# Three tiles for normed tokens and attention output, one gathered V unit, and crossings that wait in TensorE's own stream

## The chip, the cores and the metric

One NeuronCore of a Trainium2 chip runs the whole kernel. Times are device microseconds of that core. TensorE (PE) multiplies, VectorE (DVE), ScalarE (ACT) and GpSimd (POOL) work on elements, SyncE (SP) and ACT issue DMA transfers. Each engine runs its own instruction stream in order, and the streams meet at semaphores: an instruction waits until counters that other engines raise have reached a value. "PEld" in the profile is TensorE's loading of the stationary operand, "PEq", "POOLq" and so on are the sequencers that read the streams.

## The reference, cut to what matters

```python
def A(x, wqkv, wo):                       # B, S, D = 1, 2048, 448; H, Dh = 16, 28
    q, k, v = split(x @ wqkv)             # [B, H, S, Dh] each
    idx = pos[:, None] - 2 * arange(8)    # each position sees itself and 7 earlier ones, 2 apart
    logits = where(idx >= 0, einsum('bhsd,bhswd->bhsw', q, k[idx]) * Dh ** -0.5, -1e9)
    return einsum('bhsw,bhswd->bhsd', softmax(logits), v[idx]).merge_heads() @ wo

def B(x, w1, w2):                         # 448 -> 1792 -> 448
    return silu(x @ w1) @ w2

sa, ca, ga, sb, cb, gb = split(silu(c) @ w_mod, 6)
x = x + ga * A(layernorm(x) * (1 + ca) + sa)
x = x + gb * B(layernorm(x) * (1 + cb) + sb)
```

All inputs are bf16. A position only sees positions of its own parity, so the tokens are handled as two sequences of 1024 (`NP`), one for each parity, side by side.

## The kernel before

**Layout.** Activations stand transposed in SBUF: features on the partitions, positions along the free axis. The 448 features take four blocks of 128 rows (`KT`), and a parity is an index of its own. One tile, `ho` (L176), holds two things: the normed tokens `hT` in its columns 512 to 1535, and the attention output `oT` in its columns 0 to 1023. They overlap on purpose: output position 512 lies where token 0 was, once the tokens of the first half are no longer read.

**Tokens.** Chunks of 256 positions per parity are normed (`Pair`), transposed by a DMA into `hT` and scaled and shifted there (`h_later`; the `mod` operations at L236 and L238).

**Products.** A contraction over 448 is made of 64-row pieces. `pair` (L418) makes each product in two groups. The straight group (`.S`) runs two halves of TensorE's rows at once, 8 products for an output of two banks; the crossing group (`.C`), 6 products, adds the other half's pieces into the same two banks with the halves exchanged. A crossing may only start when its straight group's last product is through. `signal` (L215) sees to that: an empty instruction on GpSimd waits for that product, and the crossing's first weight load and its second product wait for GpSimd. Between a straight group and its crossing the order puts a group of another pair.

`project(k)` makes Q and K of chunk k (L483: `qk{k}{g}`, g = 0 to 3). `project_v(u)` makes V for unit u (L500: `v{u}`), 64 keys of each of two blocks, two parities: stationary operands of 64x64.

**Attention.** A unit u is two blocks of 57 queries with 64 keys each (starts in `Q0` and `K0`); there are nine. Logits (`lg{u}`, L538), exponentials on ACT (`ex{u}0`, `ex{u}1`, L545), mask on DVE (`mk{u}`, L596), product with V (`av{u}`, L612), reciprocal and normalization on DVE (`rc{u}`, `on{u}`, L619 and L624), a transposing DMA from `o` into `op` (`otr{u}`, L627), and `align` (`al{u}`, L633, L636 and L637), which copies `op` to its 114 columns of `oT`. Align of a unit that reaches past position 512 must wait until the projections have read the tokens there: the list `late` (L647).

**Output projection and FFN.** `out_proj(m)` (`wo{m}`, L663) multiplies 128 positions of `oT` by `wo`, which DVE scales by the gate ga once that is computed (L342, L345, L793); wo needs the aligns that cover its columns. Then come the second norm and the FFN (L692, L697, L717), in four chunks, and the stores.

**Order.** Every piece of work is an operation of a `Plan` with its dependencies. A table of numbers, `ORDER`, fixes the order by hand: a number is the operation's place in the list of creation, the letter its engine (p TensorE, a ACT, v DVE, g GpSimd, s SP). The framework derives semaphore waits from which instructions write and read which tile.

Of the kernel before, what the change touches and what calls it, by code (L numbers as in the profile page):

```python
# [15 lines left out]
D = 448  # L16
# [4 lines left out]
KT = 4  # L21
# [12 lines left out]
WARM, JUNK = 6, 22  # L34
HOW1 = "bbbbbbbb"
# [4 lines left out]
2a 25a 58a 59p 60a 0s 30g 33g 68v 69v 1s 26g 70g 74v 75v 76g 71v 4s 35p 54p 72a 6a 73a 39p 51s 37p 44p 42p 50p 40s 41s 9s 52s 53s 43s 3s 117v 116v  # L40
118g 77v 78a 8a 79a 110v 111v 62p 80p 83p 63v 81v 29g 84v 85v 82a 10a 5s 55s 102p 7s 119g 11a 120a 121a 47s 45s 123s 56s 112g 28g 113g 27g 64v 114v
103g 106p 115v 122s 107g 61v 67v 65v 104p 108p 49s 12s 14s 66a 98p 174v 173v 105a 109a 94p 99g 95g 175g 48s 100p 176v 167v 168v 169g 36s 46s 57s 38s
216v 170v 96p 97a 90p 91g 86p 87g 101a 15s 13s 124a 171v 127v 92p 125v 126v 88p 93v 177v 172v 178v 215v 132p 34g 133g 128p 89a 129g 31g 255p 256a 257a
130p 134p 135a 140p 131v 136p 264p 258v 137g 141g 32g 265a 16a 266a 142p 138p 210v 209v 211g 139a 143v 148p 149g 259p 150p 144p 179s 17s 180s 184a
267v 268p 260v 261v 262s 18s 145g 212g 181a 151a 269v 183v 182v 146p 156p 152p 147a 217g 157v 270v 218v 153v 219v 220v 185p 213a 214a 186g 278p 279a
280a 189p 190g 158v 281v 187p 191p 201p 188a 202g 271s 292p 192a 272v 159v 293a 203p 282p 222s 294a 221s 283v 284v 21a 193p 194g 285s 197p 195p 223v
225v 263a 204a 198g 226v 224v 199p 273p 235p 200v 274g 236g 295v 196a 306p 307a 308a 275p 276v 277v 286a 237p 238v 205p 206g 348g 349a 20s 296p 207p
287p 288g 231p 289p 232g 233p 350a 351g 297v 309v 298v 208a 299s 290v 291v 310p 243p 352g 244g 355v 247p 248g 19s 234a 356a 357a 358g 359g 245p 249p
246a 227p 311v 353v 354v 312v 320p 228g 250a 229p 300v 321a 322a 301p 239p 360v 361v 230a 302g 303p 362s 323v 305v 313s 304v 442v 251p 324p 314a 252g
253p 363s 22s 240g 23a 254a 241p 242a 325v 326v 367v 315p 154p 316g 444a 155a 334p 335a 336a 366v 364v 365v 317p 319v 392p 393g 318v 337v 384p 388p  # L50
394p 443a 338p 161v 339v 395a 385g 386p 445g 389g 390p 387a 368p 380p 327s 328v 340v 449v 381g 24s 166v 160v 163v 369g 372p 450a 451a 370p 373g 374p
382p 391a 371a 341s 329p 452g 330g 375a 383a 162v 164v 165v 376p 331p 377g 446g 378p 332v 333v 447v 405p 342a 379a 343p 344g 453g 454v 455v 414p 345p
347v 346v 406p 407p 415a 416a 417v 448v 428p 429a 430a 431v 457s 396p 397p 398p 418p 432p 515g 508g 408g 509a 516a 399g 400p 401p 402p 517a 510a 419v
433v 420v 456s 518g 519v 520v 458a 409p 511g 434v 461v 459v 512v 460v 513a 521a 514a 410p 411p 421s 474p 466p 467g 475g 422a 403v 412v 470p 471g 476p
435s 468p 477a 469a 472p 473a 462p 423p 424g 478p 479g 522s 523s 527a 463g 425p 436v 427v 426v 574v 526v 480p 481a 437p 464p 482p 438g 486p 439p 487g
465a 525a 524a 483g 484p 441v 440v 581v 485a 583a 544p 488p 545g 546p 489a 490p 532p 491p 499p 500p 492p 533g 534p 576a 575a 582a 584g 585g 586v 547a
587a 548p 549g 577g 535a 501p 528p 502g 493g 529g 578v 550p 551a 579v 580v 588s 589s 592v 404s 494p 495p 496p 552p 530p 531a 497v 503p 504p 536p 505p
622v 593a 590a 537g 538p 540p 591a 553g 506v 541g 554p 542p 539a 555a 594p 598p 595g 596p 599g 543a 597a 600p 601a 602p 565p 603g 566p 567p 604p 605a
498s 556p 568g 610p 569p 570p 614p 611g 571p 615g 572v 557p 616p 617a 612p 606p 618p 558p 607g 507s 613a 559g 619g 608p 609a 560p 620p 623p 625p 626p
621a 627p 561p 562p 563v 564s 624v 413s 573s 628g 629p 630p 631p 634p 635p 636p 637p 638p 632v 639v 640s 641v 642s 633s 643v 644a  # L60
# [81 lines left out]
def layer(ctx, tc, io, safe):  # L142
# [33 lines left out]
    ho = ct([128, 2, KT, NP + 512], "ho")  # L176
    hT = ho[:, :, :, 512:512 + NP]
    oT = ho[:, :, :, 0:NP]
# [7 lines left out]
    vb = [ct([128, 2, H, 32], f"v{i}") for i in range(NV)]  # L186
    pb = [ct([128, H * 2 * QB], f"p{i}") for i in range(NPB)]
# [7 lines left out]
    scr = ct([128, D], "scr")  # L195
# [19 lines left out]
    def signal(name, first, ends):  # L215

        def f(o):
            ends["sig"] = G.nop()
            after(ends["sig"], ends["last"])
        return P.op(name, "g", "signal", f, [first])  # L220

    P = Plan()
    for r, n in (("ps", 4 if ORDER and not safe else 3), ("v", NV), ("p", NPB), ("xn", NX), ("ob", NO), ("op", NST), ("out", 3)):
        P.resource(r, n)
# [126 lines left out]
    class Pair:  # L351

        def __init__(self, name, m, src, how, after=()):
# [12 lines left out]
            def total(o, t):  # L366
                S.activation(out=scr[:], in_=x_all[:, us[t], :], func=ACTF.Identity, accum_out=sums[:, us[t]:us[t] + 1])
# [4 lines left out]
            def square(o, t):  # L372
                S.activation(out=scr[:], in_=x_all[:, us[t], :], func=ACTF.Square, bias=mv[:, t, 0:1], accum_out=mv[:, t, 1:2])  # L373
# [44 lines left out]
    def pair(name, kind, mma, mmb, deps, evacs, mode="P", take=()):  # L418
# [3 lines left out]
        def run(o, way):  # L422
            t = ps[first["slot"]["ps"][0]]
            ks = STEPS[way]
            for n, (ka, kb) in enumerate(ks):
                stop = way == 1 and n == len(ks) - 1
                for j in ((0, 1) if way == 0 else (1, 0)):
                    hf = j if way == 0 else 1 - j
                    i = (mma, mmb)[j](t, half(hf), kb if hf else ka, way == 0 and n == 0, stop)
                    if way == 1 and n == 0 and j == 1:  # L430
                        after(i[0], ends["sig"])
            if way == 0:
                ends["last"] = i[-1]
        first = P.op(f"{name}.S", "p", kind + "S", lambda o: run(o, 0), deps, take=("ps",) + take, group=(mode, name, 0))
        sig = signal(f"{name}.g", first, ends)
        second = P.op(f"{name}.C", "p", kind + "C", lambda o: run(o, 1), [first, sig], group=(mode, name, 1))
# [10 lines left out]
    def h_first(i, nrm):  # L447
# [10 lines left out]
        def mod(o, a):  # L458
            for k in (2 * a, 2 * a + 1):
                affine(o, hT[:, :, k, 128 * i:128 * i + 128], views[a][:, k % 2], modc[:, 1, k:k + 1], modc[:, 0, k:k + 1])  # L460
# [6 lines left out]
    def h_later(k, nrm):  # L467
        trs = [nrm[i].transpose(hT[:, :, :, 256 * k + 128 * i:256 * k + 128 * i + 128].rearrange("p t k s -> p (t k) s"), ()) for i in range(2)]
        out_ = []
        for kt in range(KT):  # L470
            v = hT[:, :, kt, CP * k:CP * k + CP]
# [3 lines left out]
    def project(k):  # L475
# [3 lines left out]
        for g in range(4):  # L479
            def mm(j, g=g):  # L480
                def f(t, rows, kt, start, stop):
                    w = wp[rows, kt, H * j + 4 * g:H * j + 4 * g + 4, :].rearrange("p h d -> p (h d)")
                    return [matmul(t[:, j, :], lhsT=w, rhs=hT[rows, :, kt, s0:s0 + CP], start=start, stop=stop)]  # L483
# [10 lines left out]
    def project_v(u):  # L494

        def mm(j):
            k0 = K0[2 * u + j]

            def f(t, rows, kt, start, stop):
                return [matmul(t[half(par), j, 0:D], lhsT=hT[rows, par, kt, k0:k0 + KB], rhs=wv[rows, kt, :], start=start, stop=stop) for par in range(2)]  # L500
# [5 lines left out]
        deps = []  # L506
        for m in range(K0[2 * u] // 128, (K0[2 * u + 1] + KB - 1) // 128 + 1):
# [394 lines left out]
```

## Time and profile before

| what | us |
|---|---|
| median of 3 runs | 175.22 |
| lowest and highest | 174.96, 177.31 |
| the profiled execution | 176.32 |
| its span, first to last instruction | 174.6 |
| TensorE busy in it | 158.5 |
| mean granted TensorE clock in it | 0.967 of full |

The profile's times are those of the one profiled execution. A row of a timeline gives start, duration, engine, source line, operation, what it writes and reads, count, and in brackets the idle time before it and what ended that. A row of the waits reads "engine, output and line, what it waited for: total us, times, longest". Products overlap in TensorE, so that a product's own duration is longer than the distance to the next.

### The profile page before, as it was taken

How to read it: one execution, taken by the hardware profiler on the slowest of the kernel's cores; microseconds unless marked ns; L12 is line 12 of the kernel's file. 1: busy time of each engine (PE TensorE's matmuls, PEld its weight loads, DVE VectorE, ACT ScalarE, POOL GpSimd, SP SyncE). 2: the span in 40 equal slices, each digit the busy share in tenths (PEclk: the TensorE clock that was granted, in tenths of full speed). 3: DMA queues.
4: the chain of work that ended last, by engine and by line, in shares of the span. 5: the costliest groups of instructions: out<-in, count | busy, mean ns of one | idle time of the engine just before them, and what ended most of it. 6: DMA issues, size and time to landing. Idle time of an engine off the chain costs nothing. (4 is left out here: it accounts for less than half of the span.)

```text
span 174.6 us, 6087 instructions
## 1 busy us (share of the span) xinstructions
PE 158.5 (91%) x2684; PEld 81.8 (47%) x2684; DVE 84.2 (48%) x188; ACT 102.4 (59%) x136; POOL 24.2 (14%) x66
## 2 busy tenths in 40 slices
PE   3669999999668998999999999999999999999950
PEld 1264454655334454554456544445444444445540
DVE  3589688985573737669265950330144000202220
ACT  3348587979463587798888588786426730440000
POOL 7450432310000220030112400002200000000000
PEclk9956999999996999999999999999999999999998
DMA  4979899587930395973022462000151100000402
GB/s 139 345 252 238 169 361 130 161 109 163 168 100 4 58 193 112 307 224 60 4 63 61 59 137 54 4 0 0 29 147 53 56 0 0 4 0 0 163 31 86
DMA packets 33453, 18.51 MB, mean 106 GB/s; under 512 B 25102, under 2 KB 33422, under 8 KB 33422
## 3 DMA queue, kind: packets, MB, share of 16 engines
q1 hardware_dynamic: 30208, 14.46, 36.4%
q10 hardware_dynamic: 3214, 3.61, 6.9%
q8 instruction: 22, 0.36, 0.9%
q14 instruction: 9, 0.07, 0.2%
HBM read 10.21 MB, written 1.84 MB: 69 GB/s over the span
## 5 line engine op out<-in xcount | busy, mean ns | idle before, releaser
L697 ACT ACTIVATE both<-ps 128x1024 bf16<-128x1024 f32 x28 | 27.8, 1021 | 24.5 <-PE ps L692 24.5
L717 PE MATMUL ps<-w,both 64*128 64x448 bf16 x392 | 39.9, 349 | 0.0
L483 PE MATMUL ps<-ho,wp 64*128 64x512 bf16 x224 | 26.8, 377 | 3.4 <-ACT ho L633 3.4
L692 PEld LDWEIGHTS <-w 64*128 64x128 bf16 x392 | 19.0, 94 | 21.9
L717 PEld LDWEIGHTS <-both 64*128 64x128 bf16 x392 | 18.8, 94 | 18.2
L692 PE MATMUL ps<-wqk,w 64*128 64x512 bf16 x196 | 23.3, 376 | 0.0
L692 PE MATMUL ps<-h,w 64*128 64x512 bf16 x196 | 23.1, 376 | 0.0
L545 ACT ACTIVATE p<-ps 128x912 bf16<-128x912 f32 x18 | 15.8, 928 | 5.9 <-PE ps L538 4.4
L483 PEld LDWEIGHTS <-wp 64*128 64x128 bf16 x224 | 10.5, 94 | 16.0 <-issue 5.1
L500 PE MATMUL ps<-wv,ho 64*64 64x448 bf16 x252 | 17.1, 407 | 0.0
L671 DVE SCALAR_TENSOR_TENSOR x_all<-ps,x_all 128x448 bf16<-128x448 f32 x16 | 9.4, 623 | 15.8 <-PE ps L663 15.8
L663 PE MATMUL ps<-wo,ho 64*128 64x448 bf16 x112 | 13.3, 350 | 0.5 <-DVE ho L633 0.5
L487 ACT CAST qk<-ps 128x1024 bf16<-128x1024 f32 x11 | 11.0, 1019 | 4.4 <-PE ps L483 4.4
L395 ACT ACTIVATE xn<-x_all,nm,rs 128x512 bf16<-128x512 bf16 x12 | 9.1, 806 | 7.3 <-DVE nm L383 6.8
L373 ACT ACTIVATE scr<-x_all,mv 128x448 bf16<-128x448 bf16 x16 | 10.7, 668 | 3.3 <-POOL mv L370 3.0
L397 DVE TENSOR_SCALAR xn<-x_all,mv,rs 128x512 bf16<-128x512 bf16 x20 | 7.3, 403 | 9.9 <-POOL rs L377 9.9
L377 POOL TENSOR_TENSOR rs<-rs,negh 128x2 f32<-128x2 f32 x16 | 11.8, 735 | 1.3
L376 POOL TENSOR_SCALAR rs<-mv 128x2 f32<-128x2 f32 x16 | 3.4, 210 | 61.1 <-ACT scr L373 39.6
L363 DVE BATCH_NORM_STATS2 st<-x_all 128x6 f32<-128x448 bf16 x16 | 9.7, 606 | 3.7 <-DMA x_all<-in_A_x_dram 3.7
L752 DVE TENSOR_TENSOR wqk<-ps,x_all 128x896 bf16<-128x896 f32 x4 | 4.4, 1089 | 14.3 <-PE ps L717 12.2
L596 DVE TENSOR_TENSOR p<-p,maskb 128x1824 bf16<-128x1824 bf16 x9 | 10.0, 1113 | 2.5 <-ACT p L545 2.4
L500 PEld LDWEIGHTS <-ho 64*64 64x64 bf16 x252 | 7.7, 118 | 6.0 <-issue 2.5
(80 smaller groups left out, 147.6 us busy)
## 6 DMA issues: line engine op xcount, KB each, us to landing
both<-in_w_mod_dram SPq DMA_DIRECT2D x3, 672.0 KB, 6.2
w<-in_B_w_dram SPq DMA_DIRECT2D x3, 448.0 KB, 4.9
x_all<-in_A_x_dram ACTq DMA_DIRECT2D x2, 448.0 KB, 4.6
out_dram<-wqk SPq DMA_DIRECT2D x4, 224.0 KB, 2.0
w<-in_B_w_dram ACTq DMA_DIRECT2D x1, 784.0 KB, 7.7
w<-in_B_w_dram SPq DMA_DIRECT2D x1, 784.0 KB, 5.7
both<-in_w_mod_dram SPq DMA_DIRECT2D x3, 224.0 KB, 5.8
wo<-in_A_wo_dram ACTq DMA_DIRECT2D x1, 672.0 KB, 4.7
```

The source lines that it names most:

```text
L363: V.bn_stats(out=st[:], in_=x_all[:, us[t], :])
L373: S.activation(out=scr[:], in_=x_all[:, us[t], :], func=ACTF.Square, bias=mv[:, t, 0:1], accum_out=mv[:, t, 1:2])
L377: G.tensor_tensor(out=rs[:], in0=rs[:], in1=negh[:], op=ALU.pow)
L483: return [matmul(t[:, j, :], lhsT=w, rhs=hT[rows, :, kt, s0:s0 + CP], start=start, stop=stop)]
L487: copy_on(o)(out=qk[:, :, g, :, s0:s0 + CP], in_=t[:].rearrange("p j (t s) -> p j t s", t=2))
L500: return [matmul(t[half(par), j, 0:D], lhsT=hT[rows, par, kt, k0:k0 + KB], rhs=wv[rows, kt, :], start=start, stop=stop) for par in range(2)]
L545: S.activation(out=p_of[u][:, 2 * t * w:2 * t * w + 2 * w].rearrange("p (j n) -> p j n", j=2), in_=bank(a, t)[:, :, 0:w], func=ACTF.Exp, s ...
L596: V.tensor_tensor(out=p, in0=p, in1=m, op=ALU.mult)
L663: x = matmul(t[:, par, 0:D], lhsT=oT[rows, par, i // 2, 128 * m:128 * m + 128], rhs=wo[rows, (j + 7 - i % 2) % 7, :], start=(j == 0), stop ...
L692: return [matmul(t[:, i // 7, :], lhsT=w1[rows, kt, 128 * i:128 * i + 128], rhs=h[rows, :, kt, :], start=start, stop=stop)]
L697: S.activation(out=hid[:, k % 2, :, i, :], in_=t[:], func=ACTF.Silu)
L717: x = matmul(t[:, par, 0:D], lhsT=hid[half(hf), k % 2, jj, ii, 128 * j:128 * j + 128], rhs=w2[half(hf), ii + 7 * jj, :], start=(way == 0 a ...
```

## The change

1. The tile `ho` becomes three tiles of 512 positions for each parity: `oA` (named oa, output positions 0 to 511), `hA` (ha, tokens 0 to 511, later output positions 512 to 1023), `hB` (hb, tokens 512 to 1023). The bytes are the same.
2. V unit 4 has keys 449 to 512 and 506 to 569, on both sides of the boundary. Four copies (`hv4`) gather its columns into a tile `hv` first, both parities beside each other, and its products use stationary operands of 64x128: 14 where there were 28. The other units are in `APART` and stay as they were.
3. `signal` is gone. `crossing` puts an empty instruction into TensorE's own stream, at the head of each crossing, which waits for the straight group's last product; the weight load behind it waits for that instruction.
4. `scr`, a scratch output of the norm's sums of squares, has room for two, so two of them no longer write the same place.
5. Align 4 (output positions 456 to 569) crosses the boundary and becomes three copies.
6. `late` is shorter: an align that reaches past 512 waits for all projections of chunks 0 and 1 and V units 0 to 4 (for unit 4, its gathering).

`ORDER` is renumbered for the operations that came and went; TensorE, ACT and SP keep their order. One row of it, of the start, before and after (the signals of GpSimd, 118g and 119g there, count among the operations before):

```diff
-118g 77v 78a 8a 79a 110v 111v 62p 80p 83p 63v 81v 29g 84v 85v 82a 10a 5s 55s 102p 7s 119g 11a 120a 121a 47s 45s 123s 56s 112g 28g 113g 27g 64v 114v
+112g 77v 78a 8a 79a 104v 105v 62p 80p 83p 63v 81v 29g 84v 85v 82a 10a 5s 55s 98p 7s 113g 11a 114a 115a 47s 45s 117s 56s 106g 28g 107g 27g 64v 108v
```

TensorE's stream at the first crossing of the second half, qk23.C, and the output projection wo0.S behind it, before (`ps` is PSUM, `wp` the padded Q and K weights):

```order
L483 LDWEIGHTS wp [waits Pool_sequencer_49]
L483 MATMUL ps_110<-ho,wp 128x512 [waits Activation_49]
...
L663 LDWEIGHTS ho [waits DMAHW5_49]
L663 MATMUL ps_111<-wo,ho 128x448 [waits DVE_49]
L663 LDWEIGHTS ho
L663 MATMUL ps_111<-wo,ho 128x448 [waits DMAHW7_49]
```

And after (the empty instruction stands ahead of the first row, and its wait is shown with it):

```order
L483 LDWEIGHTS wp [waits PE_49,PE_sequencer_49]
L483 MATMUL ps_114<-hb,wp 128x512
...
L686 LDWEIGHTS oa [waits DMAHW5_49,Activation_49]
L686 MATMUL ps_115<-wo,oa 128x448 [waits DVE_49]
L686 LDWEIGHTS oa
L686 MATMUL ps_115<-wo,oa 128x448 [waits DMAHW7_49]
```

The wait for ACT moved from the crossing to the output projection, and the wait for GpSimd became one for TensorE itself.

ACT's stream at align 0, before (L487 and L505 evict projections from PSUM, L545 is the exponential, L241 issues a weight load):

```order
L545 ACTIVATE p_92<-ps_110 128x912 [waits PE_49,Activation_49]
L241 DMA w_75<-in_B_w_dram 128x2x896 [waits DMAHW3_49]
L633 COPY ho<-op_78 128x8x114 [waits DVE_49,DMAHW6_49,PE_49,Activation_49]
L505 CAST v_88<-ps_112 128x32x28
L487 CAST qk<-ps_109 128x2x2x256
```

And after:

```order
L562 ACTIVATE p_96<-ps_114 128x912 [waits PE_49,Activation_49]
L239 DMA w_75<-in_B_w_dram 128x2x896 [waits DMAHW3_49]
L655 COPY oa<-op_80 128x8x114 [waits DMAHW6_49,DVE_49]
L523 CAST v_90<-ps_116 128x32x28 [waits PE_49]
L487 CAST qk<-ps_113 128x2x2x256 [waits PE_49]
```

Align 0 no longer waits for TensorE; the evictions behind it wait for TensorE themselves, where align's wait had covered theirs.

DVE's stream around the gathering, before (L624 normalizes attention output, L345 evicts the gate ga, L397 norms tokens, L793 scales `wo`, L596 masks):

```order
L624 TENSOR_TENSOR o_96<-ps_109,rc 121x2x448 [waits DVE_49,Pool_49]
L345 CAST gbc<-ps_111 128x448 [waits PE_49,Activation_49]
L397 TENSOR_SCALAR xn_82<-x_all,mv,rs 128x512 [waits Pool_49]
L397 TENSOR_SCALAR xn_82<-x_all,mv,rs 128x512
L793 TENSOR_TENSOR wo<-wo,gbc 128x1792 [waits DMAHW5_49,DVE_49]
L596 TENSOR_TENSOR p_94<-p_94,maskb 128x1824 [waits Activation_49]
L633 COPY ho<-op_79 128x8x114 [waits DMAHW0_49,PE_49]
```

And after:

```order
L641 TENSOR_TENSOR o_100<-ps_113,rc 121x2x448 [waits DVE_49,Pool_49]
L507 COPY hv_94<-ha 128x2x4x63
L507 COPY hv_94<-hb 128x2x4 [waits DVE_49,Activation_49]
L507 COPY hv_94<-ha 128x2x4x6
L507 COPY hv_94<-hb 128x2x4x58
L343 CAST gbc<-ps_115 128x448 [waits PE_49,Activation_49]
L395 TENSOR_SCALAR xn_84<-x_all,mv,rs 128x512 [waits Pool_49]
L395 TENSOR_SCALAR xn_84<-x_all,mv,rs 128x512
L815 TENSOR_TENSOR wo<-wo,gbc 128x1792 [waits DMAHW5_49,DVE_49]
L613 TENSOR_TENSOR p_98<-p_98,maskb 128x1824 [waits Activation_49]
L655 COPY oa<-op_81 128x8x114 [waits DMAHW0_49]
```

Four copies came in ahead of the gate's eviction, and align 1 lost its wait for TensorE.

The diff, cut to its core:

```diff
-    ho = ct([128, 2, KT, NP + 512], "ho")
-    hT = ho[:, :, :, 512:512 + NP]
-    oT = ho[:, :, :, 0:NP]
+    oA, hA, hB = [ct([128, 2, KT, NP // 2], n) for n in ("oa", "ha", "hb")]
+    hT, oT = (hA, hB), (oA, hA)
...
+    hv = [ct([128, KT, 2, 2, KB], f"hv{i}") for i in range(NHV)]
...
-    scr = ct([128, D], "scr")
+    scr = ct([128, 2, D], "scr")
...
-    def signal(name, first, ends):
-
-        def f(o):
-            ends["sig"] = G.nop()
-            after(ends["sig"], ends["last"])
-        return P.op(name, "g", "signal", f, [first])
+    def crossing(ends):
+
+        ends["sig"] = T.nop()
+        after(ends["sig"], ends["last"])
...
-                S.activation(out=scr[:], in_=x_all[:, us[t], :], func=ACTF.Square, bias=mv[:, t, 0:1], accum_out=mv[:, t, 1:2])
+                S.activation(out=scr[:, t, :], in_=x_all[:, us[t], :], func=ACTF.Square, bias=mv[:, t, 0:1], accum_out=mv[:, t, 1:2])
...
+            if way == 1:
+                crossing(ends)
...
-        sig = signal(f"{name}.g", first, ends)
-        second = P.op(f"{name}.C", "p", kind + "C", lambda o: run(o, 1), [first, sig], group=(mode, name, 1))
+        second = P.op(f"{name}.C", "p", kind + "C", lambda o: run(o, 1), [first], group=(mode, name, 1))
...
+        whole = u not in APART
+        if whole:
+            def gather(o):
+                t = hv[o["slot"]["hv"][0]]
+                for j in range(2):
+                    k0 = K0[2 * u + j]
+                    for h, a, b in ((hA, k0, min(k0 + KB, 512)), (hB, max(k0, 512), k0 + KB)):
+                        if a < b:
+                            copy_on(o)(out=t[:, :, j, :, a - k0:b - k0].rearrange("p k t s -> p t k s"), in_=h[:, :, :, a % 512:a % 512 + b - a])
+            cp = P.op(f"hv{u}", "va", "hvcopy", gather, deps, take=("hv",))
+            deps = [cp]
...
+                if whole:
+                    w = hv[cp["slot"]["hv"][0]][rows, kt, j].rearrange("p t s -> p (t s)")
+                    return [matmul(t[:, j, 0:D], lhsT=w, rhs=wv[rows, kt, :], start=start, stop=stop)]
...
+            q = Q0[2 * u]
+            if q < 512 < q + 2 * QB:
+                f(out=oA[:, :, :, q:512].rearrange("p t k q -> p (t k) q"), in_=t[:, :, 0:512 - q])
+                f(out=hA[:, :, :, 0:q + QB - 512].rearrange("p t k q -> p (t k) q"), in_=t[:, :, 512 - q:QB])
+                f(out=hA[:, :, :, q + QB - 512:q + 2 * QB - 512].rearrange("p t k q -> p (t k) q"), in_=t[:, :, 64:64 + QB])
...
-        late = [x for k in chunks_of(max(0, Q0[2 * u] - 512), max(1, min(NP, Q0[2 * u + 1] + QB) - 512)) for x in qk_mm[k]] if Q0[2 * u + 1] + QB > 512 else []
-        late += [x for w in range(NU) if late and K0[2 * w] < Q0[2 * u + 1] + QB - 512 for x in v_mm[w]]
+        late = [x for k in range(2) for x in qk_mm[k]] + [x for w in range(5) for x in v_mm[w]] if Q0[2 * u + 1] + QB > 512 else []
```

The same `crossing` call stands at the head of the crossings of `out_proj` and of `ffn2`, where `signal` is dropped too.

## What the change will do to the time: a prediction

> **What bounds the kernel now.** I read the page's busy shares first, then TensorE's timeline for its gaps, then the waits that end those gaps, then the windows for the clock.
>
> The page's head and its TensorE row (busy us, share, instructions):
>
> ```profile
> span 174.6 us, 6087 instructions
> ...
> PE 158.5 (91%) x2684; PEld 81.8 (47%) x2684; DVE 84.2 (48%) x188; ACT 102.4 (59%) x136; POOL 24.2 (14%) x66
> ```
>
> TensorE (PE) is the bound: 91%, with no other engine above 59%. So the change is worth what it does to PE's idle time and clock, and nothing else unless it makes PE wait. The profiled execution took 176.32 us, 1.7 us of it around the span; it is 1.1 us above the median of the runs shown (175.22, from 174.96 to 177.31).
>
> The windows (PE busy and count, the other engines, the granted clock as PEclk):
>
> ```profile
> core 0: us, PE busy (x) PEld busy (x) DVE busy (x) ACT busy (x) POOL busy (x), PEclk, DMA share, GB/s
> 50.28:53.69 3.41, 1.41 (x16) 0.46 (x16) 1.18 (x4) 2.56 (x3) 0.00 (x0) 1.00 0.01 3
> 53.70:57.10 3.40, 3.40 (x93) 1.88 (x92) 2.07 (x3) 1.26 (x3) 0.21 (x1) 0.50 0.02 5
> 72.00:163.00 91.00, 91.00 (x1242) 44.80 (x1239) 31.27 (x71) 55.84 (x76) 7.91 (x15) 1.00 0.25 57
> ```
>
> From 72 to 163 PE is busy for 91.00 of 91.00 us: whatever is saved before 72 moves all the rest, and nothing can be saved after it. The loss lies near 50 us: a window of 3.41 us in which PE is busy for only 1.41, and right behind it 3.40 us at half clock. PE's timeline there (start, us, work, in brackets the idle time before it and what ended it):
>
> ```profile
> 43.17 2.55 PE L483 MATMUL ps<-ho,wp 64*128 64x512 bf16 x22
> 47.14 0.83 PE L483 MATMUL ps<-ho,wp 64*128 64x512 bf16 x6 [1.42 <-ACT ho L633]
> 47.79 0.94 PE L663 MATMUL ps<-wo,ho 64*128 64x448 bf16 x8
> 48.54 1.04 PE L483 MATMUL ps<-ho,wp 64*128 64x512 bf16 x8
> 49.52 0.70 PE L538 MATMUL ps<-qk 28*64 28x57 bf16 x64
> 52.90 0.82 PE L483 MATMUL ps<-ho,wp 64*128 64x512 bf16 x6 [2.00 <-ACT ho L633]
> 53.65 1.70 PE L500 MATMUL ps<-wv,ho 64*64 64x448 bf16 x16
> 65.01 0.82 PE L483 MATMUL ps<-ho,wp 64*128 64x512 bf16 x6
> 66.34 0.93 PE L663 MATMUL ps<-wo,ho 64*128 64x448 bf16 x8 [0.50 <-DVE ho L633]
> ```
>
> Three gaps: 1.42, 2.00 and 0.50 us, 3.92 together. The waits view says who held whom (total, times, longest):
>
> ```profile
> PE ps L483 <- ACT ho L633: 3.4, 2, 2.0
> DVE ho L633 <- PE ps L483: 3.1, 1, 3.1
> ACT ho L633 <- PE ps L483: 2.5, 2, 2.2
> PE ps L663 <- DVE ho L633: 0.5, 1, 0.5
> ```
>
> L633 is align, which copies attention output into `ho`; L483 reads normed tokens from `ho`. The two stand in a circle: align waits for a projection's reads, the next crossing waits for align. The first crossing, qk23.C, needs nothing that align 0 writes, nor does qk32.C need align 2: their columns of `ho` differ. These are waits on the tile's name. Only the third gap is true data: wo2.S reads what align 3 wrote, but align 3 had itself waited 3.1 us for a projection.
>
> **Part 1, three tiles.** The projections of the second half read `hb`, aligns 0 to 3 write `oa`; the circle is gone, and with it the waits in the first three rows above (the fourth follows). Term: -1.42 -2.00 -0.50 = -3.92. What is late next, gap by gap:
>
> ```profile
> 42.97 0.93 ACT L545 ACTIVATE p<-ps 128x912 bf16<-128x912 f32 x1
> 50.26 1.75 ACT L545 ACTIVATE p<-ps 128x912 bf16<-128x912 f32 x2 [1.45 <-DVE p L596]
> 51.89 0.95 ACT L633 COPY ho<-op 128x912 bf16<-128x912 bf16 x1
> 68.17 0.95 ACT L633 COPY ho<-op 128x912 bf16<-128x912 bf16 x1 [0.26 <-PE ps L483]
> 70.74 0.91 ACT L505 CAST v<-ps 128x896 bf16<-128x896 f32 x1 [1.61 <-PE ps L500]
> ```
>
> wo0.S comes to 47.79 - 1.42 = 46.37 and truly needs align 0 (0.95 us). ScalarE (ACT) is free from 43.90, so align 0 ends near 44.85: 1.5 us early. The logits L538 come to 48.10; the projection they need, qk23.C, ends at 46.55 and its 1.22 us eviction on VectorE (row below) at about 47.8: 0.3 us early, the thinnest slack. qk32.C follows at 50.89 - 1.42 = 49.47 without a gap.
>
> wo1.S truly needs align 2, whose data comes through a transposing DMA issued at 44.90 (row below); the nine take 3.5 us at the median, so about 48.4. Align 2 stands behind the two exps of L545, which follow the logits: 48.8 + 1.75 = 50.55, align 2 until 51.5. wo1.S stood at 57.19 less 3.42, and 1.7 less if the clock holds: 52.1. Slack 0.6; a transposition twice as long (7.0, landing at 51.9) would cost 0.75. wo2.S at 66.34 - 3.92 - 1.70 = 60.7 needs align 3; its transposition was issued at 58.64, and moves with its attention product (behind both gaps and half the slow stretch) by 4 us or more, to 54.6 or before: with 3.5 + 0.40 it is done at 58.5. So the 3.92 stays whole; bounds 3.2 (one such late landing) to 3.92.
>
> ```profile
> 48.01 1.22 DVE L487 CAST qk<-ps 128x1024 bf16<-128x1024 f32 x1
> ...
> 44.90 1.23 SPq L627 DMA_TRANSPOSE op<-o  x1
> 58.64 1.24 SPq L627 DMA_TRANSPOSE op<-o  x1
> op<-o SPq DMA_TRANSPOSE x9, 3.5
> ```
>
> **Part 2, the clock.** 3.40 us at 0.50 do the work of 1.70 at full clock; the stretch costs 1.70. It stands right behind the window that the 2.00 gap leaves 41% busy (1.41 of 3.41). With that gap closed every window from 46 on is full, so I take -1.70 on this execution. That the median lies 1.1 below it, and the lowest 1.4, suggests that other executions may not have paid it: a term worth 0 to 1.70 there.
>
> [...] I go by the trace, where 59% idle went ahead of the drop.
>
> **Part 3, the gathered V unit.** PE's work is the same: 28 products of 64*64 become 14 of 64*128, and four of the first run in the time of two of the second: the 55 (with one not recorded) from 60.65 below are 14 fours, (2.83 - 0.41) / 13 = 0.19 each, the 8 from 66.34 above are 4 pairs, (0.93 - 0.35) / 3 = 0.19 each, less the 0.41 and 0.35 of one product. VectorE (DVE) gets four copies between these two instructions, ahead of the cast that frees PSUM for PE's next projection:
>
> ```profile
> 36.03 1.08 DVE L624 TENSOR_TENSOR o<-ps,rc 121x896 bf16<-121x896 f32 x1
> 37.03 0.61 DVE L345 CAST gbc<-ps 128x448 bf16<-128x448 f32 x1
> 38.20 2.12 PE L483 MATMUL ps<-ho,wp 64*128 64x512 bf16 x18
> 60.65 2.83 PE L500 MATMUL ps<-wv,ho 64*64 64x448 bf16 x55
> L500 PE MATMUL ps<-wv,ho 64*64 64x448 bf16 x252 | 17.1, 407 | 0.0
> L663 PE MATMUL ps<-wo,ho 64*128 64x448 bf16 x112 | 13.3, 350 | 0.5 <-DVE ho L633 0.5
> L633 DVE COPY ho<-op x3: 339/397/402, 41.1 to 78.6; 128x912 bf16<-128x912 bf16 x3
> L636 DVE COPY ho<-op x1: 285/285/285, 103.9 to 103.9; 128x456 bf16<-128x456 bf16 x1
> ```
>
> 456 more columns cost about 0.1 us (285 to 379, the mean of L633's three), so a copy is some 190 ns and 0.2 ns a column: 8x63, 8x1, 8x6, 8x58 columns give 295, 192, 200 and 286, 0.97 together, 0.64 with the 0.08 overlap that neighbours in these rows have. The cast then ends at 37.64 + 0.64 = 38.28 where PE starts at 38.20; with the hand-over of 0.05, **+0.13**. Bounds: 0 (another bank is free first) to 0.75 (copies twice as slow for their gaps). The projection they feed, v4, runs 5 us later.
>
> **Part 4, crossings.** 68 GpSimd signals go; 68 waits enter PE's own stream, each ahead of a crossing. The rows for both, and for the products around them (min/median/max ns):
>
> ```profile
> L218 POOLq EVENT_SEMAPHORE  x68: 17/17/17, 14.5 to 158.3; - x68
> L692 PEldq EVENT_SEMAPHORE  x5: 51/51/51, 73.5 to 134.9; - x5
> L692 PE MATMUL ps<-h,w x196: 376/376/387, 74.2 to 135.7; 64*128 64x512 bf16 x196
> L692 PEld LDWEIGHTS <-w x392: 92/94/96, 74.0 to 154.7; 64*128 64x128 bf16 x196
> ```
>
> The wait now stands in front of everything PE does next. At least six products of another pair lie between a straight group's end and its crossing, three pairs of 0.19 (above) to 0.22 us (the 22 from 43.17: (2.55 - 0.38) / 10): 0.56 to 0.65 us. The chain under that cover: the last straight product 0.376, the wait 0.051, the weight load 0.094, so 0.52; before, with GpSimd's 0.017, 0.49 and two semaphore trips as now, with PE 100% busy. So the new chain is at most 0.034 longer, and if the cover was just used up, costs 68 x 0.034 = 2.3. I take 0, since five such waits of 51 ns already stand in PE's stream in the 91 us without a gap. [...]
>
> **The rest.** Freed GpSimd starts its norm steps earlier, off PE's path: 0. The doubled `scr` frees ACT of an order between two squares: 0. Align 4 in three copies instead of one adds 0 to 0.95 us on ACT; it ran 68.17 to 69.12 and ACT then idled 1.61 before 70.74, which covers it: 0.
>
> **Sum** on the profiled execution: 176.32 - 3.92 - 1.70 + 0.13 = 170.83. From the median, taken as free of the slow stretch: 175.22 - 3.92 + 0.13 = 171.43. Between the two: **171.1**.
>
> **Rivals.**
> *The next true wait.* Slack is 0.3 at the logits and 0.6 at wo1.S. A late transposition costs up to 0.75, and a new gap could again bring a slow stretch (1.70): 172 to 173.5. For it: those slacks come from subtraction. Against it: by the rows' own durations both are positive.
> *The half clock is not the gap's doing*: 176.32 - 3.79 = 172.5. [...]
> *The three tiles free nothing*: another shared name keeps the crossings waiting, 175. Against it: in the new program the crossing no longer waits for ACT.
> [...]
>
> **How the numbers follow.** Forecast 0.62, from 170.0 (0.8 lower, if the freed GpSimd and the run's spread help) to 172.2 (the 0.75 of the copies). Next true wait 0.14; crossings' 2.3 spent in part (up to 173.4) 0.07; half clock stays 0.06; frees nothing 0.05; slower 0.06. The range 170.0 to 173.5 holds all but the last two and some tail, 0.83. A measurement can tell about 2%: under 171.7 is faster, above 178.7 slower. Most of the forecast (0.57) and little of the rest (0.03) is faster: 0.60; slower 0.06; within 0.34.
>
> **What would show it.** Right: L483 without idle time before it at 45 to 50 us; no PEclk of 0.50 after 17; PE's last product near 163 where it was 168; no new idle time ahead of crossings in L692 and L717. Wrong: PE waiting for L655 (the new align) near 52 or 60; a gap ahead of L483 at 38 above 0.3; PE below 99% after 66, which would be the waits in its stream.

## The result, and the profile after

| | before | changed |
|---|---|---|
| first comparison, median us | 176.06 | 169.88 (168.65 to 170.91) |
| ratio with 95% interval | | 0.964 (0.954 to 0.975) |
| all executions of the four later series (of the changed kernel three, and its first four executions), median us | 175.69 (62 executions) | 170.47 (22 executions, 168.65 to 173.03) |
| mean granted TensorE clock over them | 0.976 | 0.985 |
| executions with a clock of 0.99 or more | 5, median 172.98 us | 6, median 170.00 us |
| profiled execution, us (span) | 176.32 (174.6) | 169.34 (167.5) |

Faster, as forecast, by more than forecast: the first median lies 0.1 us below the range. In three later series the ratio was 0.966, 0.982 and 0.985 (intervals of 0.007 to 0.011 to either side). Ratios leave out executions that stand more than 1.5% above the fastest; in the last two series these are 10 of 17 and 6 of 11 of the kernel before, all at a clock of 0.977 or less, so those two ratios hold less of the half clock than the medians, which take all executions. The first four executions of the changed kernel were also lucky: 0.6 us below the median of all 22, with a mean clock of 0.991 against 0.983 in the 18 later ones. The median of all 22 lies inside the range.

The head of the changed kernel's page and its TensorE row:

```profile
span 167.5 us, 6069 instructions
...
PE 156.1 (93%) x2670; PEld 80.5 (48%) x2670; DVE 86.1 (51%) x192; ACT 102.0 (61%) x138; POOL 25.5 (15%) x66
```

PE is busy for 2.4 us less than before, though it does the same work; the stretch at half clock behind the second gap accounts for 1.7 of that. (The kernel before also had 6.8 us at half clock at its start, from 9.3 to 16.1 us, and this execution had none there. That part comes and goes in both kernels: of the changed kernel's other three traces, one has no half clock at the start (granted clock 1.00 over the first 23.5 us), one has one stretch of it (0.93) and one has two (0.85).) Its timeline where the gaps were, and the windows around it:

```profile
42.77 2.54 PE L483 MATMUL ps<-hb,wp 64*128 64x512 bf16 x22
45.15 0.92 PE L686 MATMUL ps<-wo,oa 64*128 64x448 bf16 x8
45.90 1.03 PE L483 MATMUL ps<-hb,wp 64*128 64x512 bf16 x8
46.86 0.70 PE L555 MATMUL ps<-qk 28*64 28x57 bf16 x64
47.49 0.74 PE L686 MATMUL ps<-wo,oa 64*128 64x448 bf16 x6
48.07 0.81 PE L483 MATMUL ps<-hb,wp 64*128 64x512 bf16 x6
48.81 0.95 PE L518 MATMUL ps<-wv,hb 64*64 64x448 bf16 x16
...
50.88 0.93 PE L686 MATMUL ps<-wo,oa 64*128 64x448 bf16 x8
...
59.36 0.92 PE L686 MATMUL ps<-wo,oa 64*128 64x448 bf16 x8
```

```profile
46.00:50.00 4.00, 4.00 (x152) 2.18 (x149) 3.40 (x7) 2.40 (x3) 0.21 (x1) 1.00 0.53 136
50.00:54.00 4.00, 4.00 (x97) 1.92 (x92) 3.54 (x7) 2.36 (x7) 1.01 (x2) 1.00 0.02 4
54.00:58.00 4.00, 4.00 (x128) 2.34 (x116) 3.34 (x10) 3.61 (x7) 1.05 (x2) 1.00 0.91 205
```

No bracket, no idle time, full clock. Set against the timeline of before, product by product: the changed kernel runs 1.06 us ahead at 42.57 (its start happened to be shorter), 2.64 at qk23.C (47.14 before, 44.50 now, so 1.58 more), 4.82 at qk32.C (52.90 to 48.07, 2.18 more), 6.31 at wo1.S (57.19 to 50.88, 1.49 more), 6.98 at wo2.S (66.34 to 59.36, 0.67 more), and 6.93 from there to the last product. So from 42 us on it gains 5.87, all of it in the four places that the prediction named.

### The profile page after: what moved, and what is told of

Its sections match the earlier page's. It is cut to its first block, busy times and chain, and to the rows that moved or that the text cites. A ratio compares the mean times of both kernels' runs of the same rounds, so it can differ in the third digit from the quotient of the medians.

```text
span 167.5 us, 6069 instructions
## 1 busy us (share of the span) xinstructions
PE 156.1 (93%) x2670; PEld 80.5 (48%) x2670; DVE 86.1 (51%) x192; ACT 102.0 (61%) x138; POOL 25.5 (15%) x66
## 5 line engine op out<-in xcount | busy, mean ns | idle before, releaser
L483 PEld LDWEIGHTS <-wp 64*128 64x128 bf16 x224 | 11.0, 94 | 13.4 <-issue 3.2
L483 PE MATMUL ps<-ha,wp 64*128 64x512 bf16 x112 | 13.2, 377 | 1.1 <-DVE ha L236 1.1
L483 PE MATMUL ps<-hb,wp 64*128 64x512 bf16 x112 | 14.0, 377 | 0.0
L487 ACT CAST qk<-ps 128x1024 bf16<-128x1024 f32 x11 | 11.0, 1016 | 4.0 <-PE ps L483 4.0
L374 POOL TENSOR_SCALAR rs<-mv 128x2 f32<-128x2 f32 x16 | 3.9, 242 | 61.3 <-ACT scr L371 45.6
L774 DVE TENSOR_TENSOR ot<-ps,x_all 128x896 bf16<-128x896 f32 x3 | 3.3, 1091 | 16.1 <-PE ps L741 16.1
L641 DVE TENSOR_TENSOR o<-ps,rc 121x896 bf16<-121x896 f32 x9 | 9.7, 1078 | 0.2
```

Of the source, the lines that this page charges most:

```text
L483: return [matmul(t[:, j, :], lhsT=w, rhs=hT[k // 2][rows, :, kt, CP * (k % 2):CP * (k % 2) + CP], start=start, stop=stop)]
L487: copy_on(o)(out=qk[:, :, g, :, s0:s0 + CP], in_=t[:].rearrange("p j (t s) -> p j t s", t=2))
L641: V.tensor_tensor(out=dims(t[0:n, :], 0, (576, 2), (DH, H), (1, DH)), in0=view(bank(a))[:, :, :, 0:DH], in1=r, op=ALU.mult)
L774: V.tensor_tensor(out=t[:, p, c0:c1], in0=ps[cell["first"]["slot"]["ps"][0]][:, p, c0:c1], in1=x_all[:, 2 * m + p.start:2 * m + p.stop, c0 ...
```

## The experiments

Theory A: the gain is the three waits on one tile's name and the half clock behind the second; the crossings' waits and the gathering cost next to nothing. Against it stood that other parts of the change hold a part of the gain (B), that waits in TensorE's stream cost (C and D), and later that GpSimd's memsets collide with VectorE (E).

**All three waits put back.** In the changed kernel, semaphore waits of the old kind:

```diff
+    INS, HOLD, WAIT = {}, {'qk23': 'al0', 'qk32': 'al2'}, {'al0': 'qk22', 'al3': 'qk30'}
...
+                    if way == 1 and n == 0 and j == 1 and name in HOLD:
+                        after(i[0], INS[HOLD[name]])
...
+                if f"al{u}" in WAIT:
+                    after(INS[f"al{u}"], INS[WAIT[f"al{u}"]])
```

> The changed kernel with all three waits put back: align 0 behind the crossing of qk22 and qk23.C behind align 0, qk32.C behind align 2, align 3 behind the crossing of qk30. Theory A (these waits and the half clock behind them are the whole gain): idle times of about 1.4, 2.0 and 0.5 us in the trace, 1.42 + 2.00 + 0.50 and 3 times 0.16 = 4.4 us over the changed kernel, up to 1.5 more where the half clock falls: 174.3 to 175.8, as the kernel before. Rival (other parts of the change hold a part of the gain): under 173.5.

Measured: 176.23 us (12 executions), ratio to the kernel before 1.004 (0.9995 to 1.008), mean clock 0.973. The time is 0.4 above the upper end of what theory A expected. Its PE timeline:

```profile
46.91 0.82 PE L488 MATMUL ps<-hb,wp 64*128 64x512 bf16 x6 [1.05 <-ACT oa L660]
...
52.67 0.82 PE L488 MATMUL ps<-hb,wp 64*128 64x512 bf16 x6 [2.01 <-ACT oa L660]
...
66.11 0.93 PE L693 MATMUL ps<-wo,oa 64*128 64x448 bf16 x8 [0.56 <-DVE oa L660]
```

With three tiles, the gathering and the new crossings all in place, three waits alone bring the whole of the old time back. The rival that another part holds a net gain falls; parts of about 1 us that cancel each other are not excluded by it.

**The first wait alone** (`HOLD` with qk23, `WAIT` with al0):

> The changed kernel with the first wait put back alone: align 0 behind the crossing of qk22, qk23.C behind align 0. Theory A: idle time of about 1.4 us ahead of it, 1.4 + 0.16 = 1.6 us over the changed kernel: 171.8; the window it falls in stays above half busy, so no half clock near 50 us and a mean clock as the changed kernel's. Rival (any stall of this size brings the half clock): 173.3 and a mean clock 0.010 lower.

Measured: 171.9 us (12 executions), 1.4 above the changed kernel's 170.47 (1.3 above the 170.63 of the same series); mean clock 0.980, 0.005 below it, halfway between the two theories. The trace has one gap there, of 1.05 us where 1.4 was expected, and no half clock behind it. By time and trace, a single gap of this size costs itself and the overlap; the mean clock leaves open whether some executions paid more.

**The second wait alone** (`HOLD` with qk32):

> The changed kernel, with the second wait put back alone: the crossing qk32.C waits for align 2. Theory A: PE idle about 2.0 us ahead of it, which costs 2.0 plus the 0.16 by which neighbouring products overlap, so 2.2; and where the gap leaves one clock window under half busy, a stretch of 3.4 us at half clock behind it, 1.5 more: 172.1 to 173.6, mean clock lower by 0.010 in those executions. Rival (the half clock is not the gap's doing): 172.1 in all executions and no half clock after 20 us.

Measured: 173.44 us (6 executions, 171.78 to 178.23), 3.0 above the changed kernel (which did not run in this series); mean clock 0.976. The six fall into two groups: three with a clock of 0.977 to 0.995 took 171.78 to 172.16, and three with 0.959 to 0.970 took 174.72 to 178.23.

The profiled execution, of the first group, has the gap (2.01 us, from 48.6 to 50.6) without the half clock. In the trace of the kernel before, the clock stays at half for 3.413 us behind the second gap, and at the start for 6.827, twice as long. In the three traces that have two stretches at half clock (the kernel before, the changed kernel with all three waits put back, and the kernel before with waits in TensorE's stream, below) it is 37.55 us from the end of the first to the start of the second, 11 times 3.413. Estimated from these lengths, the clock can change once every 3.413 us; such a step of time is called a window here. Counted from the end of the half clock at the start (first row), the gap of this execution lies across a boundary. In the run with all three waits it lies inside one window (last two rows).

```profile
12.41:15.81 3.40, 3.39 (x36) 1.70 (x40) 2.62 (x9) 2.76 (x4) 0.00 (x0) 0.50 0.81 252
46.54:49.95 3.41, 2.06 (x78) 0.94 (x74) 2.73 (x6) 1.99 (x3) 0.05 (x1) 1.00 0.58 148
49.95:53.36 3.41, 2.75 (x98) 1.56 (x98) 1.60 (x3) 1.91 (x5) 1.06 (x3) 1.00 0.03 5
...
50.64:54.05 3.41, 1.40 (x24) 0.62 (x26) 1.62 (x5) 3.28 (x7) 0.26 (x2) 1.00 0.00 0
54.05:57.46 3.41, 3.41 (x90) 1.72 (x84) 2.78 (x4) 0.91 (x1) 0.85 (x2) 0.50 0.03 5
```

Split in two, the gap leaves windows that are 60% and 81% busy, and the clock stays full; in one piece it leaves one of 41%, and half clock follows. So, by these two traces, whether the gap brings the half clock depends on where it falls among the windows, which differs between executions. The first group paid 1.3 to 1.7 us for the gap. The second, whose clocks tell of more half clock but of which no trace is kept, paid 4.3 to 7.8, more than the gap and one stretch are worth; what else it paid is open.

**The gap filled with products.** The same wait, but the straight group of qk32 is computed again twice while it lasts:

```diff
+            for again in range(2 if way == 1 and name == "qk32" and not safe else 0):
+                for n, (ka, kb) in enumerate(STEPS[0]):
+                    for j in (0, 1):
+                        i = (mma, mmb)[j](t, half(j), kb if j else ka, n == 0, again == 0 and n == len(STEPS[0]) - 1)
+                ends["last"] = i[-1]
```

> As the run with the second wait put back alone, but TensorE computes the straight group of qk32 three times in all, the second and third time right ahead of its crossing, so that the 2.0 us of waiting are filled with 1.75 us of products; the result is the same. Theory A: the time of the wait stays (2.0 to 2.2 us over the changed kernel, 172.0), but no half clock follows in any execution. Rival (the half clock has another cause): half clock near 50 us as often as in the run with the empty gap.

Measured: 174.07 us (12 executions), 3.6 above the changed kernel where 2.1 was expected: a miss on the time. Mean clock 0.983, 0.002 below the changed kernel's, and no execution under 0.974 where the empty gap had three: on the clock as theory A has it, in a few executions of each. In its profiled execution PE also waited 1.7 us for tokens of the last chunk that landed late ("What is late next", below) and 0.86 us with no releaser; that is one execution, and what makes up the other 1.5 us of the median stays open.

**The gathering made twice** (`for t in hv if a < b else ():` around the copy):

> The changed kernel with the four gathering copies on VectorE made twice, the second time into an unused tile: 0.54 us more ahead of the gate's eviction. If that eviction holds up TensorE's next projection, as the prediction had it (0.13 for the first four copies), PE waits 0.5 us near 37 us and the kernel takes 0.5 longer, 170.4; if another bank is free or the copies have slack, 169.9.

Measured: 170.92 us (6 executions), 0.45 above, as expected, though six executions that spread over 2.3 us do not settle so small a difference; the trace does. VectorE's cast and PE's projection behind it, in their timelines:

```profile
38.23 0.62 DVE L343 CAST gbc<-ps 128x448 bf16<-128x448 f32 x1
...
38.90 2.34 PE L483 MATMUL ps<-hb,wp 64*128 64x512 bf16 x20 [0.51 <-DVE gbc L343]
```

The cast does hold that projection up, and the first four copies had used all the slack: of 0.54 us more copies PE waits for 0.51.

**Crossings: signals and waits exchanged.** First the kernel before, with waits in TensorE's stream (`signal` made empty, `crossing` called as in the change):

> The kernel before, one tile kept, its crossings waiting in TensorE's own stream. Theory A: same as before, ratio 1.00 within 0.005, the three idle times of 1.4, 2.0 and 0.5 us stand in the trace as they did. Theory B: 1 us or more faster. Theory C: slower, by up to 2.3 us.

Measured: 176.98 us, 1.5 above the 175.43 of the kernel before in this series, ratio 1.014 (1.007 to 1.021): slower. The three old gaps stand in its trace, and two more in PE's timeline:

```profile
44.40 0.82 PE L487 MATMUL ps<-ho,wp 64*128 64x512 bf16 x6 [0.58 <-issue]
...
75.51 1.68 PE L698 MATMUL ps<-h,w 64*128 64x512 bf16 x14 [0.48 <-issue]
```

"Issue" is idle time that nothing in the profile ends. Then the changed kernel with GpSimd's signals back, right behind each straight group:

```diff
-    def crossing(ends):
+    def signal(ends):
 
-        ends["sig"] = T.nop()
+        ends["sig"] = G.nop()
         after(ends["sig"], ends["last"])
...
             if way == 0:
                 ends["last"] = i[-1]
+                signal(ends)
```

> The changed kernel with its crossings signalled by GpSimd again. Theory A (the gain is the three waits on one tile's name and the half clock behind the second; the crossings' waits cost nothing in either place): as the changed kernel, 169.9 us, within 0.5, and PE without idle time after 32 us. Theory B (a part of the gain comes from taking the signals off GpSimd): 171 us or more. Theory C (waits in TensorE's own stream cost up to 0.034 each): up to 2.3 faster, 167.6.

Measured: 171.07 us, in theory B's range. This was no clean undoing: in its trace ScalarE waits 3.04 us for one of GpSimd's norm steps, which stood behind signals, and PE 0.61 us for ScalarE. With the signals as operations of the plan, in the places of GpSimd's stream that the kernel before had given them:

> The changed kernel with GpSimd's signals back in the places of GpSimd's stream where the kernel before had them (in the first run of this kind they stood right behind each straight group, where GpSimd's norm steps waited behind them and ScalarE for those). Theory A (the crossings' waits are worth nothing in either place): as the changed kernel within 0.5. Theory B (signals on GpSimd delay norm steps, which the changed kernel gains from): 0.5 to 1.5 slower. Theory D (waits in TensorE's own stream now and then let its fetching run dry, as the two gaps of 0.58 and 0.48 us without a releaser showed in the kernel before with such waits): 0.5 to 1.5 faster than the changed kernel, and no idle time of PE ended by issue.

> The changed kernel with GpSimd's signals back in their places, a second time. Theory A: as the changed kernel of this series within 0.5. Theory D: 0.5 to 1 faster than it again, no gap of PE ended by issue.

> The changed kernel with GpSimd's signals back in their places, beside the three: 169.3 us, all scale and shift instructions at 0.41 us. Theory E: as the run with the memsets held within 0.4. Theory D: 1 us faster than it.

Measured: 169.75, 169.25 and 169.83 us, in series in which the changed kernel itself took 170.47, 170.63 and 170.89:

> The changed kernel itself, once more, beside the other three of this series. All theories: 169.9 us, between 168.6 and 171. Where an execution's mean clock is 0.99 or more, 170.5 or less.

> The changed kernel a third time, to stand beside the other three: 170.2 us, ratio 0.966 to the kernel before. Theory D would show in it as a gap of PE ended by issue in some executions, Theory A as none.

> The changed kernel beside the two with moved memsets: 170.4 us in all theories, two scale and shift instructions at 1.17 us near 20 us.

The changed kernel's medians held these expectations; its highest times (171.44, 173.03 and 171.56) and, in the second, the ratio (0.982, not 0.966) did not. So with signals it is 0.7 to 1.4 faster in each of three series. And two waits at each crossing in place of one (`for _ in range(2):` in `crossing`):

> The changed kernel with two empty instructions instead of one in TensorE's stream at the head of each crossing, 136 in all. Theory A (they cost nothing): as the changed kernel of this series within 0.5. Theory C (each lengthens the chain under the cover of six products by 0.05): up to 68 x 0.05 = 3.4 slower, spread over the crossings. Theory D (they let the fetching run dry now and then): 0.5 to 1.5 slower, in single gaps of 0.2 to 0.9 us ended by issue.

Measured: 170.28 us, against 170.63 for the changed kernel in this series: no dearer than one, and no gap ended by issue in its trace. Here what the waits cost did not grow with their number; theory C falls, and theory D, which expected 0.5 to 1.5 more, misses here too.

**The memsets.** The traces showed another difference: without signals GpSimd reaches its memsets of `o` 2.6 us sooner. The changed kernel's GpSimd and VectorE at that time:

```profile
19.99 2.26 POOL L283 MEMSET o<- 128x1088 bf16 x2
...
19.82 2.58 DVE L236 TENSOR_SCALAR ha<-ha,modc 128x512 bf16<-128x512 bf16 x3
```

and with the signals in place (second run):

```profile
22.61 1.03 POOL L290 MEMSET o<- 128x1088 bf16 x1 [2.62 <-PE ps L489]
...
19.88 1.05 DVE L243 TENSOR_SCALAR ha<-ha,modc 128x512 bf16<-128x512 bf16 x3
```

Three VectorE instructions take 2.58 us beside the memsets and 1.05 without; PE then waited 1.05 us for those tokens in the changed kernel's profiled execution, and 0, 0.70 and 0.62 in its three other traces. Two runs tested whether this is the cost. In one the memsets of the changed kernel are held until qk10.C and qk13.C; in the other the kernel with signals has them ahead of the signals (two entries of `ORDER` moved):

```diff
+    def zero(i):
+        z = G.memset(ob[i][:], 0.0)
+        if i in LATER:
+            after(z, ENDS[LATER[i]])
```

> The changed kernel, waits in TensorE's own stream as it has them, but GpSimd's two memsets of the attention output buffers o are held until the crossings of qk10 and qk13 are through, where VectorE evicts from PSUM. Theory E (what taking the signals off GpSimd costs is these memsets: they now run at 20 to 22 us beside VectorE's scale and shift of tokens, two of whose instructions take 1.17 us in place of 0.41, and TensorE waits for those tokens): the two instructions take 0.41 again, no idle time of PE at 21 to 22.5 us, and 1.2 us less than the changed kernel, 169.2, as with the signals back. Theory D (waits in TensorE's stream let its fetching run dry): as the changed kernel, 170.4.

> The kernel with GpSimd's signals back in their places, but the two memsets of o moved ahead of the signals that held them up, so that they run where the changed kernel has them. Theory E: two of VectorE's scale and shift instructions take 1.17 us, and the time goes back to the changed kernel's, 170.4. Theory D: it stays at 169.3, since nothing waits in TensorE's own stream.

Measured: 170.20 us with the memsets held, 168.62 with signals and the memsets ahead (the changed kernel 170.89, signals in place 169.83 in the same series). VectorE's instructions moved as theory E said (1.05 us for three where held, 1.82 where ahead, so one of them was stretched there and not two). The times did not: held, it came down by 0.7 where 1.2 was expected, and six executions do not tell 0.7 from nothing; ahead, it fell by 1.2 where it should have risen by 1.1, though PE waited 0.50 us for the tokens in its trace. So theory E falls as the whole of the difference. As a part of it, it is neither shown nor excluded, and why the kernel with the memsets ahead is the faster one is open.

What is left is theory D, in part; that the fetching runs dry is an estimate in it, which no trace shows. Gaps of PE ended by issue and longer than 0.1 us stand in 7 of the 12 traces of kernels with waits in TensorE's stream and in none of the 6 with signals; over the 12 they come to 3.2 us, 0.26 each. The time from the first FFN product to the last product of all says the same: 93.97 us in five of the six traces with signals (the sixth is the first such run, with its ScalarE wait) and, within 0.01, in five of the twelve with waits; in the other seven it is 0.30 to 1.53 longer, 0.39 on the mean of the twelve. The difference in time is larger: median 170.47 of 22 executions of the changed kernel against 169.37 of 24 with signals, those with the memsets ahead among them, and 170.6 against 169.7 in the three common series without those, 18 each. That it costs about 1 us to move the crossings' waits from GpSimd's stream into TensorE's is shown. How much of it is the waits themselves, and how much the other work that GpSimd then starts sooner, is open.

The kernel with signals and the memsets ahead, at 168.62 (168.35 to 169.44), ratio to before 0.974 (0.967 to 0.980), is the fastest of all; beside it the changed kernel had 0.985 (0.977 to 0.992).

## Why the prediction came out as it did

The step that failed is the base of the sum: "From the median, taken as free of the slow stretch", and the middle of 170.83 and 171.43 behind it. Half clock was in nearly all executions of the kernel before, not in the profiled one alone: 5 of 62 had a clock of 0.99 or more, and those took 172.98 at the median, not 175.69. The mean clock rose by 0.0082 with the change (0.9764 to 0.9846); that share of 172 us is 1.4 us, which the median paid too. (Half clock at the start lowers the clock in both kernels, and 16 of 22 executions of the changed kernel are under 0.99 as well; so it is the rise of the mean that tells. A stretch of 3.4 us at half clock takes 0.0098 off the mean clock of a span of 174.6, so 0.0082 is 0.84 of a stretch on the mean of the executions.) That two executions lay 1.1 and 1.4 us below the profiled one was read as a sign that they had not paid; their clocks, which would have told, did not stand beside their times. With the term in full the prediction's sum from the median is 175.22 - 3.92 - 1.70 + 0.13 = 169.73, against 169.88 in the first comparison and 170.47 over all executions. That it comes so close is luck in part: the waits were counted 0.5 too low, the clock 0.3 too high, and about 1 us of the crossings was left out.

- *Part 1, the waits.* Right in kind and in all three places; mis-sized. It counted the idle times, 1.42, 2.00 and 0.50, and the shifts are 1.58, 2.18 and 0.67: each is 0.16 to 0.18 more. A row's idle time begins where the last product ends, but neighbours overlap: products of 0.38 us start every 0.22, so a stop also loses the overlap. 4.43 in place of 3.92.
- *What is late next.* The logits and wo1.S held their slack in the changed kernel's trace (the logits waited 0.3 us in two of the traces with signals). The thin spot was another: the last chunk's tokens, which a DMA transposes into `hb`. In the kernel before, two of VectorE's four scale and shift instructions for them waited 1.6 us for ScalarE's align; now they wait for that DMA. In the run with the memsets held:

```profile
46.72 1.38 DVE L238 TENSOR_SCALAR hb<-hb,modc 128x512 bf16<-128x512 bf16 x4 [2.92 <-DMA hb<-xn]
```

  The DMA took 6.3 us from issue to landing, and PE lost 2.0 us in three gaps; in the changed kernel's own trace it took 4.4, VectorE waited 0.3 us and PE not at all. In the run with the filled gap PE lost 1.7 us in the same way. So the rival of the next true wait shows in two traces of the experiments, though in none of the changed kernel itself, at a place that the prediction did not name.
- *Part 2, the clock.* Right: 1.70 forecast, 1.49 in the trace. A gap of 2.0 us was enough where it fell inside one window and left that 41% busy; filling it kept the mean clock at 0.983.
- *Part 3, the gathering.* Right: 0.54 us of copies for the 0.64 forecast, no slack left behind them, as the doubled copies showed; product by product the changed kernel lost 0.1 us there at most, and won it back in the V unit.
- *Part 4, the crossings.* Taken at 0, and at 2.3 if the cover was just used up; moving the waits cost about 1 us. The argument that five such waits left no gap was too thin: a cost that comes in some executions and at odd places is not seen in five places of one trace. The chance of 0.06 for slower, above 178.7, stood for a loss at every one of the 68 crossings, which no run shows: the gaps ended by issue come to 0.26 us in a trace, and two waits at each crossing took 170.28 us where one took 170.63.
- *The rest.* That freed GpSimd costs nothing is not shown: its memsets took VectorE's instructions from 0.41 to 1.17 us and made PE wait for up to 1.05 us, which the prediction had not weighed. If the time shows little of it, that was luck.

Together: 175.69 less 4.43, less 1.4, plus 1 makes 170.86, against 170.47; the 0.4 left over is open.

## What to carry to other kernels

Where two engines hold each other up over regions of one buffer that don't overlap, split the buffer at the boundary: here the waits followed the tile, not the columns touched, and 3.92 us of idle time went with the split. A stop of the bound engine cost its gap here, the 0.16 to 0.18 us by which neighbours overlap and, where it left a window 41% busy, 3.41 us at half clock. Before a sum is set against a median, find out what clock the median's executions had; one profiled execution doesn't tell. That a wait's duration is hidden does not make it free once it stands in the stream of the engine that bounds the kernel: moving the crossings' waits there cost about 1 us. And an engine that is relieved starts its other work sooner, beside something else: GpSimd's memsets, 2.6 us.

## What the runs showed of the hardware

A memset of 128x1088 on GpSimd stretched a VectorE scale and shift, SBUF to SBUF, from 0.41 to 1.17 us, the length of the memset. With the memsets ahead, an eviction from PSUM ran beside the second one and kept its 1.21 us:

```profile
20.57 2.26 POOL L290 MEMSET o<- 128x1088 bf16 x2
...
21.81 1.21 DVE L493 CAST qk<-ps 128x1024 bf16<-128x1024 f32 x1
```

In the changed kernel's trace the two stretched instructions took 1.17 us each beside memsets of 1.17 and 1.14 us; the same memset took 1.01 in the kernel before, where no scale and shift ran beside it. What held the instructions up is not shown.

The clock was at half for 3.413 us or twice that in the kernel before, and 37.55 us, 11 times 3.413, lay between its two stretches; that it changes by windows of this length is an estimate from these numbers. Around the gaps near 50 us, windows that were 41% busy (the kernel before and all three waits put back) and 54% (the kernel before with waits in TensorE's stream) were followed by half clock, and windows of 60% (the second wait alone) and 66% (the kernel before, from 43.46 us) were not. The "under half busy" of theory A was an estimate from the window of 41%; the one of 54% does not fit it. Nor does the busy share alone tell: at the start of the kernel before, a window that was 79% busy, at half clock (from 9.32 us), was followed by half clock, and in the changed kernel one of 79% at full clock (from 7.84 us) by full clock. A gap's cost so differs from one execution to the next: with the second wait alone from 171.78 to 178.23 us.
